# Three score terms in 64-row tiles instead of two passes over doubled queries, in a block-sparse attention kernel with a feed-forward layer

## The chip, the cores and the metric

The kernel runs on one core of a Trainium2 chip. The metric is the device time of one execution in microseconds (us), the median of several runs. A core has a matmul engine (PE; its weight loads are listed as PEld), a vector engine (DVE), a scalar engine (ACT), GpSimd (POOL) and a queue engine (SP) that issues most DMAs.

## The reference

Two stages. First block-sparse attention: 4 batches, 8 heads, 768 positions, head size 64, blocks of 32 (24 block rows). A block row sees its neighbours, the first and the last block, and three sampled blocks; the first and the last block row see everything. Then a gated feed-forward layer over the joined heads.

```python
scores = scale * np.matmul(q, k.transpose(0, 1, 3, 2))
mask = np.abs(blk_i - blk_j) <= window          # window = 1
mask = mask | (blk_i == 0) | (blk_j == 0) | (blk_i == n_blocks - 1) | (blk_j == n_blocks - 1)
# ... and the sampled blocks of each block row
attn = np.exp(scores - max) / (sum + 1e-09)
x = attn @ v                                    # (B*S, H*D) = (3072, 512)
g = x @ w_gate
out = (g * sigmoid(g) * (x @ w_val)) @ w_out    # d_ff = 1536, output (3072, 512)
```

All inputs and outputs are fp32.

## The kernel before, in words

**Precision.** Batch 0 computes in fp32 on PE, an instruction of which shows as two records. From batch 1 on each fp32 factor is split into a high and a low f16 part (`hi_part` on ACT, `lo_part` on DVE), and a product is made of several f16 matmuls that add up in PSUM. The feed-forward matmuls (`ffn_in`, lines 1743 and 1749, and `ffn_out`, line 1812) use the whole 128x128 array.

**Keys, before.** `load_kv` splits K of a batch and turns it by DMA transposes into `kst`, 128 partitions x 8 heads x 768 positions; of one head the 64 high parts stand on partitions 0 to 63 and the 64 low parts on 64 to 127.

**Queries, before.** The query tensor holds each head's 64 rows twice, on both halves of the partitions. `load_q` (line 874) loads a tile of 128 query positions with all of it (128x1024 fp32, `qraw`, one DMA at line 884), makes the high part on ACT and the low part in two DVE instructions (`qs`). There are 18 such tiles, six in each of batches 1 to 3. `open_q` beside it loads the rows once (`qn`, line 840) for the scale of the batch.

**Scores of the sparse blocks, before.** `block` (line 1119) handles one block row; two make a pair. DVE copies the eight key blocks that the row sees from `kst` into a ring (`kring`). Line 1157 multiplies: for two head groups and the two query parts (high, low), four matmuls of 128 contraction rows, 32 columns of weights and 256 moving columns, in four 32-column tiles of PE. As keys hold both parts on the partitions, all four combinations of parts are added. A block has its scores in one PSUM buffer (`qk`, ring of two). Then DVE masks and takes the maximum (line 1171), ACT exponentiates (line 1189), ACT and DVE split the weights (`pp`), SP transposes them by DMA, and PE multiplies with V (line 1224).

**Full rows, before.** `full_rows` (line 903) treats the first and last block row of a batch, in four steps `j` of two heads each; a step's scores (line 940) are 2 halves of the keys x 2 query parts x 4 matmuls of 384 columns. Both halves' maxima are joined before the exponentials (line 963), so that one factor scales both. Then come the split (`ppf`), two DMA transposes (line 993) and the product with V (line 1011), 48 matmuls a step.

**Chunks and order.** The work of a batch is cut into chunks of query tiles; the attention of one chunk runs beside the feed-forward of the one before. Each piece of work is a task with its engine, its needs and the buffers it takes. Their order is written out in full in the list `TURN`; every engine works through its own tasks in that order, and the kernel only asserts that it is a legal one. The costs given to `add` (such as 1.0 for a pair's scores) do not enter into the order at run time.

**Chunk 0 of batch 0** takes its query tiles by `load_whole` in `open_q0` (line 1275), 512 KB a tile, one DMA each.

Of the kernel before, what the change touches and what calls it, by code (L numbers as in the profile page):

```python
# [252 lines left out]
def tile_block_sparse_attn_swiglu(  # L253
# [620 lines left out]
    def load_q(si, g, rank):  # L874
# [4 lines left out]
        o = Tile_q()  # L879
        o.qs, o.g = qs, g  # L880
        hold = [Buf("q")]

        def load():
            nc.sync.dma_start(get(hold[0], f"qraw_{si}"), qT[b, sub])

# [17 lines left out]
    def full_rows(b, ci, sub, o, rank):  # L903
# [23 lines left out]
        for j in range(4):  # L927
# [30 lines left out]
            def power(i, j=j, c=c, qk=qk, eb=eb):  # L958
                if i == 0:
                    c["rs"] = small_t([P, 4], "rsf", f"rsf_{b}_{j}")  # L960
                    for n in range(2):
                        get(eb[n], f"ef_{b}_{j}_{n}")
# [948 lines left out]
```

## Time and profile before

| | |
|---|---|
| median of 3 runs | 777.89 us (777.6 to 779.14) |
| profiled execution, span from first to last instruction | 765.5 us |
| granted PE clock, mean | 0.993 |
| PE busy | 736.9 us (96%), 8793 matmuls |
| DVE busy | 567.3 us (74%) |
| ACT busy | 479.7 us (63%) |
| POOL busy | 240.0 us (31%) |

Of the profiled execution only the span is told; the time of a run holds what lies around it too. Engines work side by side, so busy times don't add up to the span. PE's busy time counts any moment in which a matmul is under way, also several at once in different tiles.

### The profile page before, as it was taken

To read this page: it belongs to the slowest core of one execution; us is meant where nothing else is said; L and a number is where in the kernel's file an instruction comes from. 1 tells how busy PE (TensorE), PEld (TensorE's weight loads), DVE (VectorE), ACT (ScalarE), POOL (GpSimd) and SP (SyncE) were. 2 spreads that over 40 slices of the span, in tenths; PEclk is the share of its full clock that TensorE was granted. 3 is DMA by queue.
4 is the path that set the end of the run, shared out by engine and by line. 5 is a ranking of instruction groups with operands and counts; after the bars stand their busy time and mean duration, and the time that the engine had idled before them with its cause. 6 is when DMAs were issued, how large, how long until landed. Compare 5 with 4: busy or idle time off the path is not lost.

```text
span 765.5 us, 22137 instructions
## 1 busy us (share of the span) xinstructions
PE 736.9 (96%) x8793; PEld 467.1 (61%) x8793; DVE 567.3 (74%) x1581; ACT 479.7 (63%) x1117; POOL 240.0 (31%) x290
## 2 busy tenths in 40 slices
PE   4899999999999999999999999999999999999998
PEld 3576788774686566545665566545665566555655
DVE  6999999987999998456898878647986677633220
ACT  4999655876887776745796665755764664443211
POOL 4887022222044422211343331302243333202210
PEclk9899999999999999999999999999999999999999
DMA  8856577376499996968779988787766854450001
GB/s 284 252 180 211 186 256 257 102 230 158 95 216 202 199 182 111 208 210 201 172 173 177 226 209 196 137 189 165 157 159 116 192 127 102 82 88 15 1 1 42
DMA packets 156472, 123.75 MB, mean 162 GB/s; under 512 B 113456, under 2 KB 124080, under 8 KB 156368
## 3 DMA queue, kind: packets, MB, share of 16 engines
q1 hardware_dynamic: 150736, 105.03, 57.5%
q0 software_dynamic: 5632, 17.31, 9.3%
q8 instruction: 69, 1.13, 0.6%
q14 instruction: 35, 0.29, 0.1%
HBM read 84.55 MB, written 11.01 MB: 125 GB/s over the span
## 4 chain that ended last, share of the span: by engine, by line
PE 64%; DVE 19%; ACT 5%; DMA 4%; issue 4%; POOL 1%; SPq 1%; DVEq 0%; POOLq 0%; ACTq 0%
PE p L1749 31%; PE po L1812 22%; PE qk L1157 3%; PE pv L1224 2%; DMA ptsf<-ppf 2%; DVE pp L413 1%; DVE act L1758 1%; DVE act L1763 1%; DVE w2all L451 1%; DVE w2all L452 1%; DVE kring L1135 1%; DVE e L1171 1%; PE pv L1249 1%; PE pvf L1011 1%; PE qkf L940 1%
## 5 line engine op out<-in xcount | busy, mean ns | idle before, releaser
L1749 PE MATMUL p<-xall,w1t 128*128 128x384 f16 (+1 forms) x2016 | 323.7, 319 | 1.0 <-DVE act L1758 1.0
L1749 PEld LDWEIGHTS <-w1t 128*128 128x128 f16 x2016 | 193.8, 98 | 117.0 <-issue 5.9
L1771 POOL TENSOR_TENSOR h<-act,h 128x384 f16<-128x384 f32 (+1 forms) x108 | 102.4, 952 | 333.9 <-ACT h L1768 330.4
L1812 PE MATMUL po<-w2all,h 128*128 128x512 f16 (+1 forms) x900 | 192.5, 371 | 0.3 <-DVE act L1758 0.3
L1812 PEld LDWEIGHTS <-h 128*128 128x128 f16 x900 | 86.4, 98 | 93.9 <-issue 1.6
L1145 POOL DMA_INDIRECT w2all<-vd,vidx x66 | 65.0, 985 | 92.6 <-PE pv L1224 83.1
L1743 PE MATMUL p<-xall,w1t 128*128 128x256 f32 x384 | 87.8, 383 | 3.6 <-DVE act L1758 2.5
L1758 DVE SCALAR_TENSOR_TENSOR act<-act,p 128x384 f32<-128x384 f32 (+1 forms) x108 | 54.3, 504 | 47.1 <-ACT act L1754 46.7
L1768 ACT CAST h<-act 128x384 f16<-128x384 f32 (+1 forms) x108 | 50.4, 471 | 61.8 <-DVE act L1763 61.6
L1743 PEld LDWEIGHTS p<-xall,w1t 128*128 128x128 f32 x384 | 71.0, 190 | 15.9 <-DVE act L1758 3.6
L1754 ACT ACTIVATE act<-p,gsc 128x384 f32<-128x384 f32 (+1 forms) x84 | 46.8, 558 | 52.4 <-PE p L1749 31.9
L1189 ACT ACTIVATE e<-e,nb,es 128x256 f32<-128x256 f32 x132 | 78.2, 593 | 2.2
L413 DVE SCALAR_TENSOR_TENSOR pp<-e,pp 128x512 f16<-128x512 f32 x66 | 51.0, 778 | 15.4 <-ACT pp L410 14.2
L1763 DVE SCALAR_TENSOR_TENSOR act<-act,hs,p 128x384 f32<-128x384 f32 (+1 forms) x84 | 49.4, 591 | 11.4 <-PE p L1749 9.1
L1171 DVE CUSTOM_DVE_ANT_1 e<-qk,msk 128x256 f32<-128x256 f32 x132 | 49.3, 418 | 2.5 <-PE qk L1157 2.2
L1687 POOL TENSOR_TENSOR sqx<-sqx 128x768 bf16<-128x768 bf16 (+3 forms) x18 | 22.3, 1238 | 61.0 <-ACT sqx L1683 60.4
L410 ACT ACTIVATE pp<-e 128x512 f16<-128x512 f32 x66 | 40.6, 624 | 0.6
L1135 DVE COPY kring<-kst 128x256 f16 x198 | 38.4, 253 | 3.0 <-PE qk L1157 1.5
L1644 ACT ACTIVATE ot<-po,oc 128x512 f32<-128x512 f32 (+1 forms) x25 | 16.6, 664 | 33.0 <-PE po L1812 27.3
L1519 ACT CAST xall<-pv 128x256 f16<-128x256 f32 x36 | 13.0, 364 | 36.3 <-PE pv L1249 36.3
L1157 PE MATMUL qk<-kring,qs 128*32 128x256 f16 x1056 | 35.0, 273 | 0.0
L1186 ACT ACTIVATE nb<-mx,es 128x2 f32<-128x2 f32 x66 | 19.1, 289 | 25.0 <-DVE mx L1171 24.3
(200 smaller groups left out, 991.5 us busy)
## 6 DMA issues: line engine op xcount, KB each, us to landing
stage<-in_w_dram SPq DMA_DIRECT2D x36, 512.0 KB, 6.6
w2all<-vd SPq DMA_DIRECT2D x66, 192.0 KB, 4.1
qraw<-in_q_dram SPq DMA_DIRECT2D x18, 512.0 KB, 4.5
out_dram<-ot SPq DMA_DIRECT2D x19, 256.0 KB, 2.8
qn<-in_q_dram SPq DMA_DIRECT2D x36, 128.0 KB, 4.1
stage<-in_v_dram SPq DMA_DIRECT2D x9, 512.0 KB, 5.5
vd<-stage SPq DMA_DIRECT2D x9, 512.0 KB, 2.8
stage<-in_k_dram SPq DMA_DIRECT2D x9, 512.0 KB, 6.2
```

Source lines behind the costliest of these rows:

```text
L413: nc.vector.scalar_tensor_tensor(lo, src, scale, hi, op0=ALU.mult, op1=ALU.subtract)
L1145: nc.gpsimd.indirect_dma_start(vf[0:96, 1, :], None, bt.vd, bass.IndirectOffsetOnAxis(ap=vidx[0:96, qb : qb + 1], axis=0))
L1157: nc.tensor.matmul(stv[u * BLK : (u + 1) * BLK, g].rearrange("p s k -> p (s k)"), o.q[:, l, u, g, col : col + BLK], kg[:, 2 * u + g].rearr ...
L1171: nc.vector.tensor_tensor_reduce(ev[:, g], stv[:, g], o.g.msk[:, qb, :].unsqueeze(2).broadcast_to([P, 8, BLK]), scale=1.0, scalar=-3.0e38, ...
L1189: nc.scalar.activation(ev[:, g], ev[:, g], AF.Exp, bias=nb_[:, g : g + 1], scale=o.g.es[:, 0:1], accum_out=both["rs"][:, n % 2, g : g + 1],)
L1743: nc.tensor.matmul(t[:, 0:tc_], w[:, i + 1, k_ * P : (k_ + 1) * P], x_k(k_), start=k_ == 0, stop=k_ == NKT - 1)
L1749: nc.tensor.matmul(t[:, 0:tc_], w_[:, f, m, k_, :], x_k(k_, l), start=i == 0, stop=i == 11)
L1758: nc.vector.scalar_tensor_tensor(a_, a_, 1.0, pg.tile[:, 0:tc_], op0=ALU.add, op1=ALU.mult)
L1763: nc.vector.scalar_tensor_tensor(a_, a_, sc, pw.tile[:, 0:tc_], op0=ALU.mult, op1=ALU.mult)
L1768: nc.scalar.copy(hv(f)[:, 0, :], act.tile[:, 0:tc_])
L1771: nc.gpsimd.tensor_tensor(hv(f)[:, 1, :], act.tile[:, 0:tc_], hv(f)[:, 0, :], op=ALU.subtract)
L1812: nc.tensor.matmul(po.tile[:, cs], hv(f)[:, l, ts_], w2h[:, f, m, cs], start=f == 0 and i == 0, stop=f == NF - 1 and i == 2)
```

## The change

For batches 1 to 3: keys are split into `kst` with all eight heads' high parts ahead of all low parts, so that after the transposes a 128-partition column holds two heads (64 rows each). A query tile is loaded once, as two DMAs of half the partitions (128x512), and split in one ACT and one DVE instruction. The scores are three terms (high x high, high x low, low x high; the low x low term is left out) of 64 contraction rows each: for the sparse blocks in 64x32 tiles, eight of them, for the full rows in 64x64 tiles, four of them. The two head groups of a pair of blocks go to two PSUM buffers, each of which holds both blocks. `full_rows` works in two steps `jj` of four heads and in each takes the key halves one after the other: a half has its own maximum and exponentials, and factors made from the difference of the maxima (`apart`, `factors`, `inv`) join the halves when the weights are split; the product is divided by key half. The ring `e` has four buffers (three before), `qs` three of half the size (two before). Chunk 0 of batch 0 loads its queries once as well. `TURN` is a new list.

The diff, without most of `TURN` and cut to its core:

```diff
 TURN = [
-    0, 60, 2, 1, 5, 7, 6, 22, 21, 29, 28, 3, 36, 38, 8, 4, 10, 23, 42, 9, 84, 220, ...
+    7, 0, 18, 2, 5, 22, 1, 3, 6, 21, 30, 16, 29, 28, 8, 9, 19, 38, 84, 20, 65, 23, ...
-        "qs": (work, [P, 2, 2, 4, P], F16, 2),
-        "e": (work, [P, 512], F32, 3),
+        "qs": (work, [P, 2, 4, P], F16, 3),
+        "e": (work, [P, 512], F32, 4),
...
         def load():
-            nc.sync.dma_start(get(hold[0], f"qraw_{si}"), qT[b, sub])
+            get(hold[0], f"qraw_{si}")
+            for hh in range(2):
+                sl, src = q_rows(si, hh)
+                nc.sync.dma_start(raw()[sl], src)
         def high():
-            o.q = get(qs, f"qs_{si}").rearrange("p t l j q -> p l j t q")
-            hi_part(*views(0), g.siq[:, 0:1])
+            o.q = get(qs, f"qs_{si}")
+            hi_part(o.q[:, 0], raw(), g.siq[:, 0:1])
         def low():
-            for t in range(2):
-                lo_part(lo[:, t], raw[:, t], g.siq[:, 0:1], hi[:, t])
+            lo_part(o.q[:, 1], raw(), g.siq[:, 0:1], o.q[:, 0])
+    TERMS = ((0, 0), (0, 1), (1, 0))
...
# full_rows, scores of one step and key half
+                    for n_, (ql, kl) in enumerate(TERMS):
+                        for jp in range(2):
+                            j = 2 * jj + jp
+                            for hh in range(2):
+                                hs_ = slice(hh * D, (hh + 1) * D)
+                                nc.tensor.matmul(
+                                    qk[hh].tile[jp * D : (jp + 1) * D, 0:T],
+                                    o.q[hs_, ql, j, 0 : 2 * BLK],
+                                    bt.ks.tile[hs_, 4 * kl + j, i * T : (i + 1) * T],
+                                    start=n_ == 0, stop=n_ == 2,
+                                    tile_position=(hh * D, jp * D),
+                                )
...
+            def apart(jj=jj, c=c):
+                nc.vector.tensor_tensor(m_, c["nb"][:, 0], c["nb"][:, 1], op=ALU.min)
+                for i in range(2):
+                    nc.vector.tensor_tensor(c["df"][:, i], m_, c["nb"][:, i], op=ALU.subtract)
+            def factors(c=c):
+                nc.scalar.activation(c["df"], c["df"], AF.Exp)
+            def inv(jj=jj, c=c):
+                nc.vector.tensor_tensor(c["rs"], c["rs"], c["df"], op=ALU.mult)
+                nc.vector.tensor_tensor(r_[:, 0], c["rs"][:, 0], c["rs"][:, 1], op=ALU.add)
+                recip(r_[:, 0], r_[:, 1])
+                for i in range(2):
+                    nc.vector.tensor_tensor(c["df"][:, i], c["df"][:, i], r_[:, 1], op=ALU.mult)
...
# block, scores
-            for g in range(2):
-                for l in range(2):
-                    for u in range(4):
+            for i, (ql, kl) in enumerate(TERMS):
+                for u in range(4):
+                    for g in range(2):
+                        half = slice(g * D, (g + 1) * D)
                         nc.tensor.matmul(
-                            stv[u * BLK : (u + 1) * BLK, g].rearrange("p s k -> p (s k)"),
-                            o.q[:, l, u, g, col : col + BLK],
-                            kg[:, 2 * u + g].rearrange("p s k -> p (s k)"),
-                            start=l == 0, stop=l == 1,
-                            tile_position=(0, u * BLK),
+                            st[g][u * BLK : (u + 1) * BLK],
+                            o.q[half, ql, u, col : col + BLK],
+                            kg[half, 4 * kl + u].rearrange("p s k -> p (s k)"),
+                            start=i == 0, stop=i == 2,
+                            tile_position=(g * D, u * BLK),
                         )
...
# open_q0, chunk 0
+        def load_one(si, buf):
+            view[si] = get(buf, f"q0_{si}").rearrange("p l j q -> p (l j q)").bitcast(F32)
+            for hh in range(2):
+                sl, src = q_rows(si, hh)
+                nc.sync.dma_start(view[si][sl].rearrange("p (j q) -> p j q", j=4), src)
```

The numbers in `TURN` count tasks as they are added; 2 is the load of the block table, 5, 6 and 7 are the three loads of batch 0's K, 18 the last transpose of K, 21 the first query tile, 22 the first part of V.

## Rows read from the trace of the kernel before

**Rows 1.** The core: span in us, mean granted clock of PE.

```profile
core 0: 765.5 us, clock 0.993
```

**Rows 2.** Windows: stretch, its length, busy us (instructions) of PE, PEld, DVE, ACT, POOL; clock; DMA; GB/s.

```profile
0.00:190.00 190.00, 171.18 (x1969) 127.34 (x1970) 170.17 (x380) 139.76 (x326) 80.89 (x131) 0.97 0.67 211
190.00:700.00 510.00, 503.48 (x6445) 302.46 (x6444) 385.02 (x1181) 326.34 (x766) 148.57 (x148) 1.00 0.76 162
700.00:765.50 65.50, 62.22 (x383) 37.28 (x381) 12.15 (x22) 13.63 (x25) 10.50 (x12) 1.00 0.04 13
```

**Rows 3.** The chain that ended last, share of the span by engine.

```profile
PE 64%; DVE 19%; ACT 5%; DMA 4%; issue 4%; POOL 1%; SPq 1%; DVEq 0%; POOLq 0%; ACTq 0%
```

**Rows 4.** Waits of PE, 190 to 700 us: us in total, times, longest.

```profile
PE pv L1249 <- DVE pts L1243: 3.5, 4, 1.6
PE pvf L1011 <- DMA ptsf<-ppf: 1.7, 2, 0.9
```

**Rows 5.** Groups of matmuls by line and shape: count, busy us, mean ns, idle.

```profile
L1743 PE MATMUL p<-xall,w1t 128*128 128x256 f32 x384 | 87.8, 383 | 3.6 <-DVE act L1758 2.5 <-DVE act L1763 0.9 <-ACT pts L1433 0.2
...
L1157 PE MATMUL qk<-kring,qs 128*32 128x256 f16 x1056 | 35.0, 273 | 0.0
...
L940 PE MATMUL qkf<-kst,qs 128*32 128x384 f16 x192 | 10.1, 327 | 0.0
```

**Rows 6.** Timeline of PE: start, us until its last matmul ends, line, what, count.

```profile
405.75 0.86 PE L1224 MATMUL pv<-w2all,pts 128*32 128x128 f16 x64
406.44 1.05 PE L1157 MATMUL qk<-kring,qs 128*32 128x256 f16 x32
407.42 2.12 PE L1812 MATMUL po<-w2all,h 128*128 128x512 f16 x9
...
432.31 1.06 PE L1157 MATMUL qk<-kring,qs 128*32 128x256 f16 x32
433.19 0.85 PE L1224 MATMUL pv<-w2all,pts 128*32 128x128 f16 x64
433.98 4.06 PE L1812 MATMUL po<-w2all,h 128*128 128x512 f16 x18
```

**Rows 7.** Timeline of PE in batch 0, fp32 scores of a pair.

```profile
24.95 1.09 PE L1388 MATMUL qk<-w1t,q 64*32 64x256 f32 x32
25.97 0.34 PE L1404 MATMUL qk<-dupm,ones_h 128*128 128x192 bf16 x2
```

**Rows 8.** Timeline of PE at scores of full rows.

```profile
466.80 0.82 PE L940 MATMUL qkf<-kst,qs 128*32 128x384 f16 x16
467.56 4.07 PE L1749 MATMUL p<-xall,w1t 128*128 128x384 f16 x24
...
473.73 0.83 PE L940 MATMUL qkf<-kst,qs 128*32 128x384 f16 x16
474.39 0.69 PE L1011 MATMUL pvf<-ptsf,stage 128*32 128x128 f16 x48
```

**Rows 9.** The query tiles (qraw): count, min/median/max ns, first and last start, shape.

```profile
L413 DVE SCALAR_TENSOR_TENSOR qs<-qraw,siq,qs x36: 739/747/1397, 147.0 to 609.7; 128x512 f16<-128x512 f32 x36
L884 SPq DMA_DIRECT2D qraw<-in_q_dram x18: 328/408/534, 122.2 to 602.9; - x18
L410 ACT ACTIVATE qs<-qraw,siq x18: 1132/1144/1152, 144.3 to 607.4; 128x1024 f16<-128x1024 f32 x18
```

**Rows 10.** A high part of K, 128x512, on ACT; same columns.

```profile
L410 ACT ACTIVATE stage<-stage,ks x18: 706/719/723, 175.9 to 512.0; 128x512 f16<-128x512 f32 x18
```

**Rows 11.** Issues of query loads of half the partitions (qn); same columns.

```profile
L840 SPq DMA_DIRECT2D qn<-in_q_dram x36: 542/607/1704, 90.9 to 479.4; - x36
```

**Rows 12.** Timeline of PE at the start: the transposes of batch 0's K.

```profile
7.05 5.35 PE L593 MATMUL kT<-ident,w1t 128*128 128x128 f32 x24 [7.05 <-DMA w1t<-in_k_dram]
```

**Rows 13.** Timeline of PE at a full-row product in batch 1.

```profile
309.63 0.44 PE L1011 MATMUL pvf<-ptsf,stage 128*32 128x128 f16 x24
310.90 0.44 PE L1011 MATMUL pvf<-ptsf,stage 128*32 128x128 f16 x24 [0.84 <-DMA ptsf<-ppf]
```

More of the change, by code (lines that the diff above doesn't have):

```diff
@@ L881, in load_q, with raw @@
         hold = [Buf("q")]
+        def raw():
+            return hold[0].tile[:, 0:512].rearrange("p (j q) -> p j q", j=4)
         def load():
-            nc.sync.dma_start(get(hold[0], f"qraw_{si}"), qT[b, sub])
-        def views(l):
-            return qs.tile[:, :, l], hold[0].tile.rearrange("p (j t q) -> p t j q", j=4, t=2)
+            get(hold[0], f"qraw_{si}")
+            for hh in range(2):
+                sl, src = q_rows(si, hh)
+                nc.sync.dma_start(raw()[sl], src)
         def high():
-            o.q = get(qs, f"qs_{si}").rearrange("p t l j q -> p l j t q")
-            hi_part(*views(0), g.siq[:, 0:1])
+            o.q = get(qs, f"qs_{si}")
+            hi_part(o.q[:, 0], raw(), g.siq[:, 0:1])
         def low():
-            (lo, raw), hi = views(1), views(0)[0]
-            for t in range(2):
-                lo_part(lo[:, t], raw[:, t], g.siq[:, 0:1], hi[:, t])
-        need = [g.scaled, add("SP", 0.501, load, [], rank, behind=g.loaded, take=hold, dma=1.35)]
-        t = add("ACT", 0.95, high, need, rank, take=[qs], use=hold)
-        o.done = add("DVE", 1.33, low, [t], rank, use=hold + [qs])
+            lo_part(o.q[:, 1], raw(), g.siq[:, 0:1], o.q[:, 0])
+        need = [g.scaled, add("SP", 1.3, load, [], rank, behind=g.loaded, take=hold, dma=1.5, many=2)]
+        t = add("ACT", 0.63, high, need, rank, take=[qs], use=hold)
+        o.done = add("DVE", 0.68, low, [t], rank, use=hold + [qs])
         return o
+    TERMS = ((0, 0), (0, 1), (1, 0))
     def full_rows(b, ci, sub, o, rank):
@@ L975, in full_rows @@
+            eb = [[Buf("e") for _ in range(2)] for _ in range(2)]
             x = []
             for i in range(2):
-                x.append(in_turn("exp", "ACT", 0.66, lambda i=i, f=power: f(i), m, rank, take=[] if i else eb,
-                             use=[qk[i]] + (eb[1:] if i else [])))
-            full_exp[0] = x[1]
-            r = add("DVE", 0.45, inv, x, rank)
-            there, turned = [], []
-            for i in range(2):
-                pp, pts = Buf("pp"), Buf("pts")
-                turned.append(pts)
-                def high(i=i, j=j, c=c, pp=pp, eb=eb):
-                    hi_part(get(pp, f"ppf_{b}_{j}_{i}")[:, 0:T], eb[i].tile[:, 0:T], c["rs"][:, 3:4])
-                def low(i=i, c=c, pp=pp, eb=eb):
-                    lo_part(pp.tile[:, T : 2 * T], eb[i].tile[:, 0:T], c["rs"][:, 3:4], pp.tile[:, 0:T])
-                def turn(i=i, j=j, pp=pp, pts=pts):
-                    nc.sync.dma_start_transpose(
-                        get(pts, f"ptsf_{b}_{j}_{i}")[:, 0:768].rearrange("p (m q) -> p m q", q=P), pp.tile[:, 0:768]
-                    )
-                a = in_turn("high", "ACT", 0.5, high, [r], rank, take=[pp], use=[eb[i]])
-                a = in_turn("low", "DVE", 0.54, low, [a], rank, use=[pp, eb[i]])
-                there.append(add("SP", 1.27, turn, [a], rank, take=[pts], use=[pp], dma=1.3))
@@ L1001, in product @@
-            def product(j=j, turned=turned):
-                if j == 0:
-                    get(pv, f"pvf_{b}")
-                for c6 in range(6):
-                    i, cc = divmod(c6, 3)
-                    pq = turned[i].tile[:, 0:768].rearrange("p (l c u q) -> p l c u q", l=2, u=2, q=D)
-                    vv = vbuf[c6 // 2].tile.bitcast(F16).rearrange("p (t l h d) -> p t h l d", h=H, l=2, d=D)[:, c6 % 2]
-                    for l, w in ((0, P), (1, D)):
-                        for n in range(4):
-                            hh, at = n // 2, n % 2 * BLK
-                            nc.tensor.matmul(
-                                pv.tile[n * BLK : (n + 1) * BLK, j * P : j * P + w],
-                                vv[:, 2 * j + hh, l, at : at + BLK],
-                                pq[:, 0 : w // D, cc, hh, :],
-                                start=c6 == 0 and l == 0,
-                                stop=c6 == 5 and l == 1,
-                                tile_position=(0, n * BLK),
-                            )
@@ L1020, in full_rows, with scores @@
-            pvs.append(in_turn("pv", "PE", 0.681, product, there + vl, rank, take=[] if j else [pv],
-                               use=turned + vbuf + ([pv] if j else [])))
+                plan.key = f"f{ci}.{jj}.{i}"
+                qk = [Buf("qk"), Buf("qk")]
+                def scores(i=i, jj=jj, qk=qk):
+                    for hh in range(2):
+                        get(qk[hh], f"qkf_{b}_{jj}_{hh}_{i}")
+                    for n_, (ql, kl) in enumerate(TERMS):
[7 more added lines that the diff above has]
+                                    bt.ks.tile[hs_, 4 * kl + j, i * T : (i + 1) * T],
+                                    start=n_ == 0,
+                                    stop=n_ == 2,
+                                    tile_position=(hh * D, jp * D),
+                                )
@@ new lines, in full_rows @@
+                s = in_turn("qk", "PE", 0.49, scores, [o.done] + bt.k_done, rank, take=qk, use=[o.qs, bt.ks])
+                m = [in_turn("top", "DVE", 0.47 + 0.16 * hh, lambda hh=hh, f=top: f(hh), [s, tsc], rank, use=[qk[hh]]) for hh in range(2)]
+                for hh in range(2):
+                    x.append(in_turn("exp", "ACT", 0.66, lambda hh=hh, f=power: f(hh), m, rank, take=[eb[hh][i]], use=[qk[hh]]))
+            full_exp[0] = x[-1]
+            plan.key = f"f{ci}.{jj}"
+            def apart(jj=jj, c=c):
+                c["df"] = small_t([P, 2, 2], "df", f"df_{b}_{jj}")
+                m_ = small_t([P, 2], "mf", f"mf_{b}_{jj}")
+                nc.vector.tensor_tensor(m_, c["nb"][:, 0], c["nb"][:, 1], op=ALU.min)
+                for i in range(2):
+                    nc.vector.tensor_tensor(c["df"][:, i], m_, c["nb"][:, i], op=ALU.subtract)
@@ new lines, in full_rows, with high, low, turn @@
+            r = add("DVE", 0.46, apart, m, rank, behind=x[0])
+            r = add("ACT", 0.25, factors, [r], rank)
+            r = add("DVE", 0.92, inv, [r] + x, rank)
+            for i in range(2):
+                plan.key = f"f{ci}.{jj}.{i}"
+                there, turned = [], []
+                for hh in range(2):
+                    pp, pts = Buf("pp"), Buf("pts")
+                    turned.append(pts)
+                    def high(hh=hh, i=i, jj=jj, c=c, pp=pp, eb=eb):
+                        hi_part(get(pp, f"ppf_{b}_{jj}_{hh}_{i}")[:, 0:T], eb[hh][i].tile[:, 0:T], c["df"][:, i, hh : hh + 1])
+                    def low(hh=hh, i=i, c=c, pp=pp, eb=eb):
+                        lo_part(pp.tile[:, T : 2 * T], eb[hh][i].tile[:, 0:T], c["df"][:, i, hh : hh + 1], pp.tile[:, 0:T])
+                    def turn(hh=hh, i=i, jj=jj, pp=pp, pts=pts):
+                        nc.sync.dma_start_transpose(
+                            get(pts, f"ptsf_{b}_{jj}_{hh}_{i}")[:, 0:768].rearrange("p (m q) -> p m q", q=P), pp.tile[:, 0:768]
+                        )
+                    a = in_turn("high", "ACT", 0.5, high, [r], rank, take=[pp], use=[eb[hh][i]])
+                    a = in_turn("low", "DVE", 0.54, low, [a], rank, use=[pp, eb[hh][i]])
+                    there.append(add("SP", 1.27, turn, [a], rank, take=[pts], use=[pp], dma=1.3))
+                def product(i=i, jj=jj, turned=turned):
+                    f0 = not (i or jj)
+                    if f0:
+                        get(pv, f"pvf_{b}")
+                    for cc in range(3):
+                        c6 = 3 * i + cc
+                        vv = vbuf[c6 // 2].tile.bitcast(F16).rearrange("p (t l h d) -> p t h l d", h=H, l=2, d=D)[:, c6 % 2]
+                        for jp in range(2):
+                            j = 2 * jj + jp
+                            for l, w in ((0, P), (1, D)):
+                                for n in range(4):
+                                    hh, at = n // 2, n % 2 * BLK
+                                    pq = turned[hh].tile[:, 0:768].rearrange("p (l c u q) -> p l c u q", l=2, u=2, q=D)
+                                    nc.tensor.matmul(
+                                        pv.tile[n * BLK : (n + 1) * BLK, j * P : j * P + w],
+                                        vv[:, 2 * j + hh, l, at : at + BLK],
+                                        pq[:, 0 : w // D, cc, jp, :],
+                                        start=f0 and cc == 0 and jp == 0 and l == 0,
+                                        stop=jj == 1 and c6 == 5 and jp == 1 and l == 1,
+                                        tile_position=(0, n * BLK),
+                                    )
+                f0 = not (i or jj)
+                pvs.append(in_turn("pv", "PE", 0.681, product, there + vl, rank, take=[pv] if f0 else [],
+                                   use=turned + vbuf + ([] if f0 else [pv])))
@@ L1111, in attention @@
                 first = [next(x) for x in two]
-                qks = [x[2] for x in first]
-                a = in_turn("qk", "PE", 1.0, lambda first=first: [x[1]() for x in first], [x[0] for x in first] + [o.done], r,
-                            take=qks, use=[o.qs])
+                a = in_turn("qk", "PE", 0.65, lambda first=first: [x[1]() for x in first], [x[0] for x in first] + [o.done], r,
+                            take=both["qk"], use=[o.qs])
                 for x in two:
@@ L1301, in open_q0 @@
                 load_v0(rank)
-            if whole:
-                o.qs = Buf("qs") if not ci else None
-                o.done = add("SP", 0.5, lambda si=si, x=o.qs: load_whole(si, x), [], rank + 0.2 * sub, take=[o.qs] if o.qs else [], dma=1.45)
+            if not ci:
+                o.qs = Buf("qs")
+                o.done = add("SP", 1.3, lambda si=si, x=o.qs: load_one(si, x), [], rank + 0.2 * sub, take=[o.qs], dma=1.5, many=2)
+                o.q0 = lambda u, hh, si=si: view[si][hh * D : (hh + 1) * D, u * P : (u + 1) * P]
+            elif whole:
+                o.qs = None
+                o.done = add("SP", 0.5, lambda si=si: load_whole(si), [], rank + 0.2 * sub, dma=1.45)
                 o.q0 = lambda u, hh, si=si: view[si][hh * D : (hh + 1) * D, (2 * u + hh) * P : (2 * u + hh + 1) * P]
```

92 lines of the change are left out of this document (33 added, 59 removed), and 284 rows, old and new, of the table TURN.

## The prediction, made before the changed kernel was run

> **What bounds the kernel now.** I read the span and clock first: one core, 765.5 us at a granted clock of 0.993 [rows 1], so the clock gives nothing back. The runs' median is 777.89 us; I carry the 12.4 us that lie around the profiled span over unchanged and make the sum on the span. Then the table of busy time by stretch [rows 2]: from 190 to 700 us, where batches 1 to 3 run beside the feed-forward matmuls, PE is busy 503.5 of 510 us. It idles 6.5 us there, against 18.8 us in the first 190 us (batch 0, whose arithmetic the change leaves alone) and 3.3 us after 700. The chain that ended last is PE for 64% [rows 3]. The waits of PE in the middle stretch add up to about the same 6 us; the longest kinds are transposes that wait for DVE (3.5 us) and full-row products that wait for their transposed weights (1.7 us) [rows 4]. So from 190 us on a microsecond of PE occupancy is a microsecond of the end, and what other engines gain is worth at most those 6.5 us. A busy PE still hides what a matmul costs, so I take costs from starts: the distance from one group's first matmul to the start of the next group on PE.
>
> **Scores of the sparse blocks.** There are 1056 matmuls of 256 columns, 32 to a pair of blocks, so 33 pairs; the full rows have 192 of 384 columns, 12 groups of 16 [rows 5]. A pair's 32 stand in four-wide column tiles of 128 rows, that is 8 passes of 256 columns. Before a product (same tile shape) a pair takes 433.19 - 432.31 = 0.88 us, or 0.110 a pass; before a whole-array matmul 407.42 - 406.44 = 0.98 us [rows 6]. The change makes 3 terms x 4 x 2 = 24 matmuls a block in 64-row tiles, eight side by side: 6 passes a pair. That eight 64x32 tiles do run side by side is visible in batch 0: 32 fp32 records of 256 columns take 25.97 - 24.95 = 1.02 us up to a whole-array matmul [rows 7]. In the whole array such a record takes 87.8 / 384 = 0.229 us [rows 5], so 32 of them in fours would be 8 x 0.229 = 1.8 us; 1.02 less a 0.1 us change of shape is 4 passes of 0.23. For f16 I take a pass at 0.110, so 0.66 us a pair: 0.22 less, x 33 = -7.3 us.
>
> **Scores of the full rows.** Now 16 matmuls a head pair in 4 passes: 474.39 - 473.73 = 0.66 us before a product, 467.56 - 466.80 = 0.76 before a whole-array matmul [rows 8], so 0.165 a pass. New: 12 groups of 12 matmuls in 64x64 tiles, four side by side, 3 passes each: 0.495, i.e. 0.165 less, x 12 = -2.0 us. The product matmuls keep their number (48 a group, 12 groups); they are only divided by key half instead of by head pair.
>
> **The price of changing tile shape.** Today scores and products have the same 32-column shape, so where they stand back to back nothing is paid; a step to the whole array costs 0.98 - 0.88 = 0.10 us [rows 6], 0.76 - 0.66 = 0.10 [rows 8], and for a product 433.98 - 433.19 = 0.79 against 406.44 - 405.75 = 0.69, again 0.10 [rows 6]. Counted along PE's timeline, 10 of 33 pairs stand right before a product and 16 right behind one, and 8 and 6 of the 12 full-row groups: 40 boundaries (two of them in [rows 6]). In the new kernel scores are 64-row and products 128-row, so each of these becomes a change of shape. No row shows an f16 step between two partial shapes: bounds 0 (the column tiling stays, nothing drains) and 0.22 (a step out and a step in). I take 0.11, by the nearest rows: 40 x 0.11 = +4.4 us, if the new order has as many such neighbours. The Trainium skill, page "TensorEngine Tiling (Array Packing)", section "Key Properties", says that changing the tiling mode, unlike changing the tile, drains the engine; by that rule the 40 boundaries cost what a step to the whole array does and this term stays at +4.4, without it it is 0 and the forecast is 768.1 us. The trace shows the drain towards the whole array alone.
>
> **Queries.** Each of 18 query tiles is now loaded once, 128x512 instead of 128x1024. ACT: 1.144 us [rows 9] becomes about the 0.719 of a 128x512 part of K [rows 10], 18 x 0.425 = 7.6 us less. DVE: 36 low parts of 0.747 [rows 9] become 18, 13.4 us less. SP: one issue of 0.408 us [rows 9] becomes two of 0.607 [rows 11], 18 x 0.81 = 14.5 us more on a queue where, behind a load, stand transposes of later blocks; PE has feed-forward matmuls before it needs them, and if that cover were gone a late transpose would cost 0.8 us once. Full rows, for each of six steps: DVE has 11 small operations where two head pairs had 10, ACT one more of about 0.3 us, so even; they lie beside PE's feed-forward. The key rows change their places only: the copies into the ring keep shape and number, priced at nothing for the same cover. What relief on DVE and ACT is worth is bounded by 0 and the 6.5 us of PE idle [rows 2]. I take -1.0, nearer to 0, since DVE loses 13 us of 385 in that stretch and what is late next are the product's transposes.
>
> **The order.** It is written out for every task, so each idle moment may move. PE's first matmul waits 7.05 us for K, and the 24 transposes take 5.35 us because they follow its parts [rows 12]. The new list puts K's third part ahead of the block table but a part of V ahead of K's second: bounds -0.4 (one SP issue) and +2.5 us (512 KB at the 211 GB/s of [rows 2]); the query tiles of chunk 0, 0.5 MB less, come behind. I take +0.5. Elsewhere 0, with -6.5 (no idle left in the middle) to +6 (twice as much).
>
> **Sum:** -7.3 - 2.0 + 4.4 - 1.0 + 0.5 = -5.4 us; span 760.1, time 772.5 us.
>
> **Rivals.**
> (a) The new order closes the gaps and keeps scores from products: -9.3 - 6.5 + 0.5 = -15.3, 762.6 us. For it: the waits of [rows 4] are few and single, and 40 boundaries can be sorted. Against: 6.5 of 510 us is already little. I count to it all below 768.
> (b) The changes of shape eat the gain: 40 x 0.22 = +8.8, so 9.3 - 8.8 leaves about 0: 778 us. For it: drains in and out are separate costs. Against: the steps to the whole array show 0.10 once.
> (c) Slower: the joining of halves. Nothing of a full-row step may be scaled before all four of its exponentials are done, so scores, maxima and exponentials of a second half (0.5 + 2 x 0.55 + 2 x 0.86 us by the durations of today's) and some 0.9 us of factors come before the first product, 4 us more latency in each of six steps, while the ring of four exponential buffers is all taken, so sparse blocks behind it stop too. If PE has 2 us a step uncovered, +12 - 5.4 = +6.6: 784.5 us. It decides from 0.9 us a step on. For it: products already wait for transposes (310.90, 0.84 us idle [rows 13]). Against: those are two waits in twelve groups, 1.7 us in all [rows 4], and feed-forward matmuls are there to stand between.
> (d) What counts is the matmul, not its columns: today's 32 start 0.88 / 32 = 27 ns apart on average; if that were a floor, 48 take 1.32 us, +0.44 x 33 = +14.5, and with -2.0 + 4.4 + 0.5 it is 795 us. Against: 64 products start within 406.44 - 405.75 = 0.69 us, 11 ns apart [rows 6]. The same time comes out if 64-row f16 tiles ran only four wide, which [rows 7] speak against. The Trainium skill, "TensorE: Matmul & The Clock Gate", section "Wait — 56ns, not 53.3ns?", gives a floor of about 25 ns from start to start however few the columns; by that figure (an estimate) 48 matmuls would take 1.2 us, and the time would be near 791 us. This trace's 11 ns differ from it, for column tiles.
>
> **How the numbers follow.** Forecast (768 to 776.3): 0.54. (a) 0.20, (b) 0.09, (c) 0.13, (d) 0.04. About 0.2%, 1.6 us, is what a measurement can tell from no change. Faster 0.54 + 0.20 = 0.74; same 0.09; slower 0.17. The range runs from 764 (most of (a) lies above) to 780 (the near part of (c)); some 0.2 is left out.
>
> **What would show it.** Right: a pair of scores at about 0.66 us from start to start before the same shape and 0.76 before others, full-row groups at 0.50 to 0.60, 48 and 12 matmuls a group, starts in bursts of eight; a product behind scores costing about 0.1 more than today; PE busy in the middle some 5 us shorter, idle there still 4 to 8 us. Wrong: pairs at 0.85 or more (d), PE waits at full-row products or blocks behind them above 5 us (c), idle near 0 (a), or the first 190 us longer by more than 2 us.

## The result, and the profile after

The changed kernel took 768.60 us (median of 4 runs, 767.14 to 772.53) against 778.33 us (777.60 to 779.14) for the kernel before beside it: ratio 0.9889, interval 0.9868 to 0.9911, so 9.7 us less. In two later comparisons the ratio was 0.989 both times (0.9854 to 0.9926 and 0.9858 to 0.9923), with the kernel before at 769.5 and 770.1 us. The two kernels keep their ratio while the level moves by over 1% from one comparison to another; hence every experiment below is read by its ratio to the kernel before that ran beside it.

The level matters for one reading. The two profiles of before and after have the same span, 765.5 [rows 1] and 765.2 us, and from them alone nothing was gained. They come from different levels: a run of the changed kernel whose span is 765.2 took 767.14 us, 1.9 more, and in a later run of the kernel before the difference is 2.3 (before_again), so the execution behind the 765.5 of before must have taken about 768 us and not 777.89. A repeat of the changed kernel beside a kernel before of 770 us has a span of 757.6 us (after_anchor, below). Where the two kernels are compared by their time on PE, I use repeats of one level.

The cores view and the windows of the changed kernel, with the columns of [rows 2]:

```profile
core 0: 765.2 us, clock 1.000
```

```profile
0.00:190.00 190.00, 169.56 (x1968) 126.93 (x1969) 165.48 (x379) 139.59 (x327) 76.46 (x131) 1.00 0.68 204
190.00:700.00 510.00, 501.53 (x6929) 295.37 (x6927) 367.53 (x1169) 318.99 (x772) 141.82 (x148) 1.00 0.71 155
700.00:765.50 65.50, 61.63 (x380) 36.88 (x377) 12.24 (x22) 13.22 (x25) 9.94 (x11) 1.00 0.04 13
```

In the middle stretch DVE's busy time fell from 385 to 368 us and ACT's from 326 to 319; PE is as full as it was, with 484 matmuls more. The chain that ended last goes over PE even more than in [rows 3], and DVE's part of it went from 19% to 8%:

```profile
PE 77%; DVE 8%; DMA 5%; ACT 4%; issue 4%; DVEq 0%; SPq 0%; POOL 0%; ACTq 0%; POOLq 0%
```

The waits of PE from 190 to 700 us (total, times, longest), to set against [rows 4]:

```profile
PE qk L1184 <- issue: 1.8, 5, 0.4
PE pv L1250 <- issue: 1.7, 5, 0.5
PE pv L1275 <- DVE pts L1269: 1.6, 2, 1.0
```

The transposes' wait for DVE is down from 3.5 to 1.6 us, and the full-row products, for which rival (c) foretold 12 us of waits, are gone from the top of the list. New at the top is "issue", in which PE waited for nothing that the profile shows, at scores and products of the sparse blocks.

The two score groups (busy us, mean ns, idle before), to set against [rows 5]:

```profile
L1184 PE MATMUL qk<-kring,qs 64*32 64x256 f16 x1584 | 30.4, 271 | 3.4 <-issue 1.8 <-DVE mx L1197 1.1 <-DVE kring L1157 0.3
L945 PE MATMUL qkf<-kst,qs 64*64 64x384 f16 x144 | 8.2, 331 | 0.0
```

PE's timeline at a pair of blocks ahead of a product, at one ahead of the whole array, and at two groups of full rows (start, us to the last end, count):

```profile
247.22 0.85 PE L1184 MATMUL qk<-kring,qs 64*32 64x256 f16 x48
248.00 0.86 PE L1250 MATMUL pv<-w2all,pts 128*32 128x128 f16 x64
...
360.76 0.85 PE L1184 MATMUL qk<-kring,qs 64*32 64x256 f16 x48
361.54 0.66 PE L1782 MATMUL p<-xall,w1t 128*128 128x384 f16 x3
...
456.00 0.68 PE L945 MATMUL qkf<-kst,qs 64*64 64x384 f16 x12
456.61 0.44 PE L1275 MATMUL pv<-ident,pts 128*128 128x128 f32 x2
...
463.96 0.68 PE L945 MATMUL qkf<-kst,qs 64*64 64x384 f16 x12
464.57 0.66 PE L1782 MATMUL p<-xall,w1t 128*128 128x384 f16 x3
```

A pair takes 248.00 - 247.22 = 0.78 us ahead of a product and 361.54 - 360.76 = 0.78 ahead of a whole-array matmul; before it was 0.88 and 0.98 [rows 6]. A full-row group takes 0.61 us; before 0.66 and 0.76 [rows 8]. The query tile's rows, to set against [rows 9] (count, shortest/median/longest ns, first and last start):

```profile
L888 SPq DMA_DIRECT2D qraw<-in_q_dram x36: 542/594/792, 134.6 to 579.9; - x36
L410 ACT ACTIVATE qs<-qraw,siq x18: 705/710/722, 144.2 to 614.1; 128x512 f16<-128x512 f32 x18
L413 DVE SCALAR_TENSOR_TENSOR qs<-qraw,siq,qs x18: 733/746/1434, 150.1 to 623.4; 128x512 f16<-128x512 f32 x18
```

### The profile page after: what moved, and what is told of

Read it like the earlier page. It is cut to its first block, busy times and chain, and to the rows that moved or that the text cites. A ratio compares the mean times of both kernels' runs of the same rounds, so it can differ in the third digit from the quotient of the medians.

```text
span 765.2 us, 23107 instructions
## 1 busy us (share of the span) xinstructions
PE 732.7 (96%) x9273; PEld 459.2 (60%) x9273; DVE 545.2 (71%) x1569; ACT 471.8 (62%) x1123; POOL 228.2 (30%) x290
## 4 chain that ended last, share of the span: by engine, by line
PE 77%; DVE 8%; DMA 5%; ACT 4%; issue 4%; DVEq 0%; SPq 0%; POOL 0%; ACTq 0%; POOLq 0%
PE p L1782 38%; PE po L1845 22%; PE qk L1184 4%; PE pv L1250 3%; PE p L1776 3%; DMA stage<-in_w_dram 2%; DMA pts<-pp 1%; DMA w1t<-in_k_dram 1%; PE pv L1275 1%; PE pv L1481 1%; PE qk L1421 1%; PE pvf L1032 1%; DVE w1t L452 1%; ACT e L1452 1%; PE qkf L945 1%
## 5 line engine op out<-in xcount | busy, mean ns | idle before, releaser
L1804 POOL TENSOR_TENSOR h<-act,h 128x384 f16<-128x384 f32 (+1 forms) x108 | 94.9, 882 | 357.8 <-ACT h L1801 357.5
L413 DVE SCALAR_TENSOR_TENSOR pp<-e,pp 128x512 f16<-128x512 f32 x66 | 45.8, 705 | 12.0 <-ACT pp L410 10.8
L1156 DVE COPY kring<-kst 128x256 f16 x198 | 40.1, 259 | 1.3 <-PE qk L1184 0.8
L1184 PE MATMUL qk<-kring,qs 64*32 64x256 f16 x1584 | 30.4, 271 | 3.4 <-issue 1.8
L1250 PE MATMUL pv<-w2all,pts 128*32 128x64 f16 (+1 forms) x2112 | 29.6, 207 | 2.7 <-issue 1.7
```

What stands on the lines that cost most here:

```text
L1184: nc.tensor.matmul(st[g][u * BLK : (u + 1) * BLK], o.q[half, ql, u, col : col + BLK], kg[half, 4 * kl + u].rearrange("p s k -> p (s k)"), ...
L1250: nc.tensor.matmul(to[rows_, g, 0:w_], pq[:, g, l, cc, u], vg[:, cc, 0:w_, 2 * u + g, :], start=i == 0, stop=i == 3, tile_position=(0, u * ...
L1804: nc.gpsimd.tensor_tensor(hv(f)[:, 1, :], act.tile[:, 0:tc_], hv(f)[:, 0, :], op=ALU.subtract)
```

## The experiments

Three questions were open: whether the 9.7 us are the change's at all, given two equal spans; which term brings them; and what the new waits called "issue" are. "The kernel before" means the one beside it. A difference between two experiments is the difference of their ratios times 770 us.

**before_again, after_again, after_anchor: is the gain real?** The two kernels unchanged.

> The kernel before, unchanged, to see a second profiled execution. The profile before has a span of 765.5 us, 12.4 us under the median of its runs (777.9), while the changed kernel's span is only 2 us under its own time (765.2 and 767.1). Theory A: the span before belongs to an execution that was itself some 10 us quicker than the median; then a second profile has a span near 776 us and shows where PE idles 10 us more. Rival B: some 12 us of the kernel before lie outside its span in every run; then the second span is again near 765.5 us, and the gain lies outside the instructions. Time: 777.6 to 779.2 us either way.

> The changed kernel, unchanged, beside the kernel before on one chip. In the first comparison it was 9.7 us quicker, but a second run of the kernel before took 768 us with the same code, so part of that may be the chip. Theory A (the gain of some 10 us is real): 0.987 of the kernel before. Theory B: in the profiles the stretch from the first output matmul to the end takes 594.5 us in both kernels; the columns saved at the scores (9 us) are spent again, about 3 us on changes of tile shape and 6 us on gaps of up to 0.7 us in long unbroken runs of small matmuls, where PE waits for nothing that the profile shows; then 0.995 to 1.0 of the kernel before.

> The changed kernel once more, so that the three beside it are compared with it on the same chip. Expected 0.989 of the kernel before, as in the last comparison.

Measured: before_again 769.90 us, ratio 1.0007 (0.9987 to 1.0027), span 767.4; after_again 760.88, 0.9890; after_anchor 760.13, 0.9890, span 757.6. The gain is real, 8.5 us by the ratio. What before_again was expected to show came neither way: its time is not 777.6 to 779.2 us, and span and time differ by 2.3 us, so neither did PE idle 10 us more nor do 12 us lie outside the span. Between the first and the last start of the feed-forward's output matmuls lies everything that PE does beside them. The rows of those matmuls (count, ns, first and last start) in before_again, then after_anchor:

```profile
L1812 PE MATMUL po<-w2all,h x900: 272/379/390, 169.7 to 763.9; 128*128 128x512 f16 x166, 128*128 128x256 f16 x14
```

```profile
L1845 PE MATMUL po<-w2all,h x900: 272/379/391, 166.9 to 753.8; 128*128 128x512 f16 x166, 128*128 128x256 f16 x14
```

594.2 became 586.9, 7.3 us less (the kernel before beside them was at 768 and 770 us). Summed by kind, from each start to the next on PE (a wait counts to what stands before it): pair scores -4.4, full-row scores -1.1, full-row products -1.9, sparse products +3.2, block transposes +0.7, feed-forward -3.7.

**after_4terms: does a pass of columns set the time?** The left-out term is put back, 16 matmuls more a pair and 4 more a full-row group.

```diff
-    TERMS = ((0, 0), (0, 1), (1, 0))
+    TERMS = ((0, 0), (0, 1), (1, 0), (1, 1))
-                                    stop=n_ == 2,
+                                    stop=n_ == 3,
...
-                            stop=i == 2,
+                            stop=i == 3,
```

> The changed kernel with a fourth term (low x low) in all scores: 64 matmuls a pair and 16 a full-row group, eight and four passes as before the change, with everything else of the change kept. Theory A: a pass is 0.107 us, so 2 x 33 passes of it and 12 of 0.16 give +9 us, 777.6 us. Rival B (the order or the loads are the gain, and PE has slack at the scores): +4 us or less, under 773 us. If PE runs short of instructions in these dense stretches, more than +9.

Measured: 770.79 us, ratio 1.0025 (1.0008 to 1.0043). Against 0.989 that is 10.4 us more, for 66 passes of 256 columns and 12 of 384, which at 0.107 and 0.16 us make 9.0 us. A pair in its profile:

```profile
362.93 1.07 PE L1184 MATMUL qk<-kring,qs 64*32 64x256 f16 x64
363.93 0.50 PE L1782 MATMUL p<-xall,w1t 128*128 128x384 f16 x2
```

Eight passes take 363.93 - 362.93 = 1.00 us where six took 0.78, so 0.11 a pass, and a column added to PE is paid in full at the scores. The 10.4 us are not columns alone, though: this profile also has three stops called "issue", 3.3 us in all, of the kind that before_split explains below, while other waits are shorter.

**before_cols and after_halfcols: is a column taken away a gain in full?** In the kernel before, the query's low part multiplies only the first half of the key columns: 9.0 us of columns less, with shape, loads and order untouched. In the changed kernel the second and third term of the sparse blocks do so: 7.0 us less. Both leave part of the scores out.

```diff
+                        ns = 4 if l else 8
-                            kg[:, 2 * u + g].rearrange("p s k -> p (s k)"),
+                            kg[:, 2 * u + g, 0:ns].rearrange("p s k -> p (s k)"),
```

```diff
-                            kg[half, 4 * kl + u].rearrange("p s k -> p (s k)"),
+                            kg[half, 4 * kl + u, 0 : 4 if i else 8].rearrange("p s k -> p (s k)"),
```

> The kernel before with its own order, in which the low query part is multiplied with the first half of the key columns alone (this part of the scores is left out): the scores take 25% fewer PE columns, as in the change, but keep the number of matmuls, the 32-column tiles of 128 rows and the doubled queries. Theory A (PE's columns are the gain): 0.21 us less a pair and 0.16 a full-row group, 9 us in all, so about 769 us, and as no tile shape changes it could be 4 us better than the change without its other gains. Rival B (the new order and the lighter loads are the gain): above 774 us.

> The changed kernel in which the second and third score term of the sparse blocks take the first half of their key columns alone (these parts are left out): as many matmuls, 4 instead of 6 passes of columns a pair, 0.21 us less a pair, 7 us in all by columns. Theory A (columns set the time): -7 us against the changed kernel. Theory B (in long runs the number of instructions sets it): the clean pairs gain their 0.21 us, but the runs of 112 matmuls stay as long as they are, so -3 to -5 us.

Measured: before_cols 765.41 us, ratio 0.9968 (0.9945 to 0.9990), only 2.5 us; after_halfcols 756.15, 0.9830 (0.9802 to 0.9857), 4.6 us better than 0.989; with the spread of both ratios (some 3.5 us either way) that does not decide between the 7 and the 3 to 5 that were expected. In the kernel before, PE met DVE instead. Its longest waits from 166 to 705 us in before_again, then in before_cols:

```profile
PE pv L1249 <- DVE pts L1243: 2.6, 4, 1.6
...
PE p L1749 <- DVE act L1758: 1.0, 3, 0.5
```

```profile
PE pv L1251 <- DVE pts L1245: 4.9, 4, 1.9
PE p L1751 <- DVE act L1760: 2.6, 5, 0.9
```

The profile of before_cols is of one of its quickest runs, so I compare what lies between the first and last output matmul, 594.2 us in before_again and here:

```profile
L1814 PE MATMUL po<-w2all,h x900: 272/379/390, 166.5 to 756.1; 128*128 128x512 f16 x166, 128*128 128x256 f16 x14
```

That is 589.6 us, 4.6 less, and of the 4.4 that are missing from 9.0, 3.9 stand in the two rows of waits. DVE came close behind PE: columns taken away without relief of DVE are worth between a quarter (2.5 us by the ratio) and a half (4.6 in the two profiles) of their 9.0 us.

**after_qfull and after_low2: what is the lighter query load worth?** after_qfull puts back the 512 KB load, the 1024-column high part on ACT and two low parts on DVE, with everything else as changed (half of the query rows hold other heads' values). after_low2 makes the low part twice and does nothing else.

```diff
-            get(hold[0], f"qraw_{si}")
-            for hh in range(2):
-                sl, src = q_rows(si, hh)
-                nc.sync.dma_start(raw()[sl], src)
+            nc.sync.dma_start(get(hold[0], f"qraw_{si}"), qT[b, sub])
-            hi_part(o.q[:, 0], raw(), g.siq[:, 0:1])
+            hi_part(o.q.rearrange("p l j q -> p (l j q)"), hold[0].tile, g.siq[:, 0:1])
-            lo_part(o.q[:, 1], raw(), g.siq[:, 0:1], o.q[:, 0])
+            for _ in range(2):
+                lo_part(o.q[:, 1], raw(), g.siq[:, 0:1], o.q[:, 0])
```

```diff
-            lo_part(o.q[:, 1], raw(), g.siq[:, 0:1], o.q[:, 0])
+            for _ in range(2):
+                lo_part(o.q[:, 1], raw(), g.siq[:, 0:1], o.q[:, 0])
```

> The changed kernel with the old load of a query tile from batch 1 on: 512 KB in one DMA, a high part of 1024 columns on ACT, two low parts on DVE (the values of the second half of the partitions are those of other heads). It undoes the lighter query load alone. Theory A (hidden beside PE): +0 to +1.5 us, 768.6 to 770. Rival B (DVE and ACT set part of the end): +4 us or more.

> The changed kernel with the low part of each query tile made twice on DVE (18 instructions of 0.75 us, 13.4 us of DVE time more), the rest of the lighter query load kept. Undoing the whole lighter load cost some 4.5 us by the two comparisons with the kernel before. If DVE alone is behind that: +3 to +4.5 us against the changed kernel. If it was ACT or the loads' bytes: +0 to +1.5.

Measured: after_qfull 764.50 us, ratio 0.9948 (0.9925 to 0.9970), 4.5 us worse than 0.989; after_low2 762.66, 0.9901 (0.9871 to 0.9931), 0.8 us worse, with some 3.4 us of spread either way. The lighter load is worth about 4.5 us, as rival B said. How much of that DVE's 13 us bring is not settled: 0.8 is told apart neither from nothing nor from the 3 that were expected of DVE alone, and between the first and last output matmul after_low2 takes 589.1 us and after_qfull 591.1, against 586.9 in after_anchor, so 2.2 against 4.2 us. Whether ACT's time or the bytes bring the rest was not tried.

**before_split: does the number of matmuls cost, apart from columns?** In the kernel before, each sparse score matmul is cut in two of half the columns: 1056 matmuls more, with the same columns, tile shape, order and loads.

```diff
-                    for u in range(4):
+                    for w, u in ((w, u) for w in range(2) for u in range(4)):
+                            sw = slice(4 * w, 4 * w + 4)
-                            kg[:, 2 * u + g].rearrange("p s k -> p (s k)"),
+                                kg[:, 2 * u + g, sw].rearrange("p s k -> p (s k)"),
```

> The kernel before, where each score matmul of the sparse blocks is two of half the columns: 64 instead of 32 matmuls a pair (1056 more), the same columns, tiles, order and results. By columns alone: +0 to +1 us. Theory B (instructions run short in long unbroken runs of small matmuls; 16 of 33 pairs stand right behind products here): gaps appear there, 0.5 to 1 us each, +6 to +12 us.

Measured: 776.83 us, ratio 1.0091 (1.0059 to 1.0124), 7.0 us worse, as theory B had it. The profile is of its slowest run (782.64 us). PE's timeline at one place, in before_again and then in before_split (the bracket is idle time and what ended it):

```profile
230.84 1.06 PE L1157 MATMUL qk<-kring,qs 128*32 128x256 f16 x32
231.72 0.85 PE L1224 MATMUL pv<-w2all,pts 128*32 128x128 f16 x64
```

```profile
230.95 1.08 PE L1159 MATMUL qk<-kring,qs 128*32 128x128 f16 x64
231.85 0.62 PE L1226 MATMUL pv<-w2all,pts 128*32 128x128 f16 x41
234.81 0.47 PE L1226 MATMUL pv<-w2all,pts 128*32 128x64 f16 x23 [2.34 <-issue]
```

The 64 half-size matmuls take 231.85 - 230.95 = 0.90 us where 32 took 0.88, so the number costs nothing there; but of the 16 pairs that stand right behind products, nine take longer than the others, 1.09 to 3.07 us. What costs here is that the products behind them stop after 64 + 41 = 105 matmuls without a pause, for 2.34 us, for nothing that the list of waits names; 32 + 64 = 96 went through.

The trace's DMA records say what this stop waited for. One DMA queue is called "instruction" (packets, MB, share of 16 engines):

```profile
q8 instruction: 77, 1.26, 0.7%
```

These are 77 packets of 16,384 bytes for the 19,769 weight loads, matmuls and waits that the trace records on PE, 257 to a packet; in the changed kernel it is 72 packets for 18,618. So this queue brings PE its own program. The packet nearest to the stop began at 232.35 us, when PE had just started its last matmul, and landed at 233.59; PE went on 1.2 us later, at 234.81. The other two waits of before_split called "issue" between output matmuls (2.0 and 1.1 us) end 1.2 and 1.3 us after such a packet landed, and the three stand whole multiples of 256 records apart. These stops are waits for the next piece of the program: matmuls in small parts use it up faster. The three stops of after_4terms stand at such places too, 1.3 to 1.5 us behind a packet.

The first profile of the changed kernel has shorter stops:

```profile
208.16 0.86 PE L1250 MATMUL pv<-w2all,pts 128*32 128x128 f16 x64
208.95 0.51 PE L1184 MATMUL qk<-kring,qs 64*32 64x256 f16 x19
209.72 0.31 PE L1184 MATMUL qk<-kring,qs 64*32 64x256 f16 x3 [0.26 <-issue]
210.46 0.63 PE L1184 MATMUL qk<-kring,qs 64*32 64x256 f16 x26 [0.43 <-issue]
211.02 1.70 PE L1782 MATMUL p<-xall,w1t 128*128 128x256 f16 x14
```

This pair, right behind 64 products, takes 211.02 - 208.95 = 2.07 us instead of 0.78; it stops after 64 + 19 = 83 matmuls. In this profile 29 of the 33 pairs are free of it. No packet of the program was on its way here (the nearest ran from 201.96 to 203.28 and from 210.72 to 211.68 us), so what this pair waited for stays open. And the number in a row does not make a stop by itself: after_again and after_anchor run the same list, with up to 144 small matmuls in a row, and have no wait called "issue" between their first and last output matmul.

**after_spread, after_cut10, after_cut3: can the order break the runs?** Only `TURN` differs: 26, 10 and 3 groups of feed-forward matmuls are pulled forward between scores and products that stand side by side. One of the places, in after_cut3:

```diff
-    2221, 2053, 2054, 2055,
+    2054, 2221, 2053, 2055,
```

> The changed kernel with 26 changes in the order alone: wherever scores and products of batches 1 to 3 would make a run of more than 64 small matmuls on PE, the next feed-forward matmul group is pulled between them (in three places the small group is moved behind it instead). Theory B (long runs of small matmuls starve PE of instructions): the gaps go from the middle of the runs, 15 to 22 us of lost time in runs of small matmuls become some 9, and the kernel gains 4 to 8 us over the changed kernel, although some 20 further changes of tile shape cost 2 us. Theory C (the gaps are waits for weights or data, which move along): no gain, or 1 to 2 us lost by the added changes of shape.

> The changed kernel with 10 changes in the order: in ten runs of more than 100 small matmuls (scores and products of sparse blocks back to back) the next feed-forward group is pulled into the run, only where no transpose of a block's output comes closer to its product than three such groups, or than it was. With 26 such changes and no such rule the kernel was 21 us slower than the changed one, as PE then waited for data at transposes and products. Theory B (long runs starve PE of instructions, and the loss of the 26 came from data waits alone): 0.5 to 1 us a run back, less 0.1 for one more change of shape, so 3 to 8 us quicker than the changed kernel. Theory C (any group pulled forward makes data late, and the gaps are not instructions): 2 to 8 us slower.

> The same with three changes, in the runs of more than 112 small matmuls alone. Theory B: 1 to 3 us quicker than the changed kernel; theory C: 0 to 3 us slower.

Measured: after_spread 782.01 us, ratio 1.0154 (1.0118 to 1.0191), 21 us worse than the changed kernel beside it, outside both expectations; after_cut10 764.58, 0.9932 (0.9909 to 0.9956), 3 us worse; after_cut3 761.48, 0.9881 (0.9853 to 0.9909), no difference. PE's longest waits from 166 to 705 us in after_spread:

```profile
PE pv L1269 <- DVE pts L1263: 7.4, 5, 2.3
PE pvf L1026 <- DMA ptsf<-ppf: 3.1, 3, 2.2
PE pv L1244 <- DMA w2all<-vd: 2.7, 2, 1.4
```

By these waits the feed-forward group that I pulled forward was the cover of a later transpose or product. These three settle that such moves don't help here, not that shorter runs would not: no order was found that cut the runs and left every cover in place.

## Why the prediction was right, and where not

**The mechanism held.** PE's time in the middle set the end, the scores' columns were the main term, and the kernel became faster by a little more than forecast: 8.5 to 9.7 us where 5.4 was worked out. The first measured time, 768.60, lies 0.6 us above the 768 below which I counted everything to rival (a); that it fell on this side is luck, for the runs of one kernel spread by more.

**Pairs, -7.3, and full rows, -2.0: right for an undisturbed group.** A pair is at 0.78 us, where 0.66 and one change of shape make 0.76 to 0.77; a full-row group is at 0.61, just above the 0.50 to 0.60 that I named. after_4terms gives 0.11 a pass, as I took it. Summed over the middle, the pairs' row shows only 4.4 of the 7.3: ten more of them pay a change of shape (33 instead of 23, 1.1 us), and in after_anchor five take 0.86 to 1.30 us instead of 0.78, 1.4 us more. With products and changes of shape in, the small matmuls of the middle are 4.3 us shorter, where -7.3 - 2.0 + 4.4 = -4.9 was worked out.

**Changes of shape, 0.11 each: right.** The pair costs 0.78 us ahead of the whole array and ahead of a product of another partial shape alike, so both steps cost the same, 0.12 to 0.13 by a pass of 0.109 (from the starts within it) to 0.110, and not the 0.22 of rival (b). The step back, from 64 products to scores, costs 208.95 - 208.16 = 0.79 us where 0.69 was the price without a change [rows 6], again 0.10. The Trainium skill, page "TensorEngine Tiling (Array Packing)", section "Key Properties", says that any change of mode drains the engine; the two equal 0.78 agree. The count was 40 and the new order has 30 such boundaries: 20 at pairs and 10 at full-row groups. With the other kinds, changes of shape between the first and the last output matmul went from 110 to 144, 34 x 0.1 = +3.4 us against my +4.4.

**Relief of DVE and ACT, -1.0: the mis-sized term.** I bounded it by PE's 6.5 us of idle and took a value near 0, since DVE lost only 13 of 385 us. Undoing the query load alone cost 4.5 us, within the bound and far from -1.0. Outside the small matmuls the middle became 3.0 us shorter (feed-forward -3.7, transposes +0.7). before_cols shows the same from the other side: with DVE as it was, 9.0 us of columns less bring 2.5 to 4.6. The step that failed is "a microsecond of PE occupancy is a microsecond of the end": true for work added, and only in part for work removed, because another engine is close behind. The parts of the change need each other, so their gains do not add as separate terms: columns alone bring 2.5 to 4.6 of 9.0 us, and without the lighter load the whole change brings 4.0 of 8.5.

**Not foreseen: stops in runs of small matmuls.** From start to start, the scores and products of the middle take 75.6 us in before_again, 71.4 in after_anchor and 76.2 in the first profile of the changed kernel. Their columns, at 0.107 us for 256, are 62.9, 53.9 and 53.9 of that, so 12.7, 17.4 and 22.3 are left over, waits and changes of shape included. The 34 further changes of shape account for 3.4 of the 4.7 between the first two, so some 1.3 us is left at that level, and 6 in the first profile, where stops called "issue" take 4.0. Most of what separates that profile from after_anchor (594.3 and 586.9 us in the middle) is therefore in the small matmuls. Two kinds of stop have to be kept apart. Those of before_split and after_4terms are shown to be waits for the program, by the packets of the instruction queue: three of 77 came too late in before_split. The Trainium skill, page "Runtime: NRT & Kernel Launch", section "Instruction fetch mechanics", says that an engine's instructions are fetched in blocks of 256 while it runs, and calls the cost mostly hidden; the 257 records to a packet agree, and a stop of 2.34 us is not hidden. The cause of the shorter stops in the first profile of the changed kernel is open; they are gone in two repeats.

**The start, +0.5, and 12.4 us around the span.** The first output matmul starts between 166 and 172 us in executions of either kernel, so a step of 0.5 us can't be read. The 12.4 us were no constant: span and time differ by 2 to 3 us in every later run, and the rest was the level. It did no harm, for it stands in both times alike.

**Rivals.** (c) fell: no full-row product waits in the list of the changed kernel, so the joining of halves found its cover. (d) fell: 48 scores start within 0.78 us, 16 ns apart. (b) fell with the price of the step between two partial shapes. (a), gaps closed and neighbours sorted, was partly so: the boundaries are 30 instead of 40, and the feed-forward is 3.7 us shorter from start to start, by order or by relief, which no run separates; but PE did not stop idling, with 4.1 us of 539 in after_again where before_again has 6.2. The measured gain lies between the forecast and it.

## What to carry to other kernels

When one engine is busy 98% of a stretch, price work added to it in full and work removed from it only down to the next engine; a before-only experiment that takes the columns away and nothing else tells how far that is. Count instructions as well as columns: where PE waits for nothing that the list of waits names, look whether a packet of the queue "instruction" landed just before it went on, as at all three such stops of before_split. Look at more than one profile before such a stop is put down to the kernel: the changed kernel had eleven in one profile and none in two others. Compare spans only within one comparison, since the level of one and the same kernel moved by 1.3% (778.3 and 768.1 us), more than this change was worth.

## What the runs showed of the hardware

Splitting matmuls cost nothing within the group (64 in 0.90 us, 32 in 0.88), and 2.34 us in the next group, in whose row one would not look for it: PE had used up its instructions, and went on 1.2 us after the next 16,384 bytes of them had landed. Eight 64x32 tiles of f16 run side by side at the pace of four 128x32 tiles: a pass of 256 columns took 0.109 us by its starts, as before the change. A step between two partial tile shapes costs what a step to the whole array costs, 0.10 to 0.13 us (a pair takes 0.78 us ahead of either).
